# Attention scores in whole float32 products, a third turned buffer, and a new order

## The chip, the cores and the metric

The kernel runs on one core of a Trainium2 chip. The metric is the device time of one execution in microseconds (us). Three runs of the kernel before took 922.01, 923.61 and 915.67 us; the median is 922.01. The engines are TensorE (PE, with its weight loads as PEld), VectorE (DVE), ScalarE (ACT), GpSimd (POOL) and SyncE (SP), which issues the DMAs. Each works through its own queue in order.

## The reference

The inputs are q, k and v of 8 batches, 8 heads, 576 positions and 64 dimensions, and the weights of a gated MLP. All is float32.

```
scores = (q @ k^T) / sqrt(64)
thresh = max(scores, axis=-1) - tau
scores = where(scores >= thresh, scores, -1e9)
attn   = exp(scores - max(scores));  attn = attn / (sum(attn) + 1e-9)
x      = attn @ v                      # heads side by side: (8, 576, 512)

h = gelu_tanh(x @ w_in);  u, v = halves of h
v = layer_norm(v) * g_ln
g = u * (w_sg @ v + b_sg)              # w_sg mixes the 576 positions
out = x + g @ w_out
```

The threshold makes the scores delicate: a score close to the threshold is kept or dropped whole, so the products of q and k are made to float32 precision.

## The kernel before

The work is 32 pairs of heads (`attention(n)`, a pair n is two heads of a batch) and 8 batches of the MLP (`moe(b)`, after each four pairs). Every operation is recorded as a step in a plan, and a list of numbers, `ORDER`, says in which order the steps are issued; `PLACES` says which of the 8 banks of PSUM a step takes. The order of issue is the order in each engine's queue. Attention of later pairs is woven into the MLP of earlier batches.

In a pair, the queries are cut into four blocks of 128 for each head (i = 0 to 3) and a tail of 64 for both heads together (i = 4). A step of scores (`scores`, L583 to L594) writes two heads at once: head 0 from partitions 0 to 63 of q and k, head 1 from 64 to 127, in two halves of 288 keys each. It takes four banks. The tail step (`tail_scores`, L596) uses a copy of q's tail with zeros, so that 128 rows hold both heads, and takes two banks.

For 31 of the pairs q and k are split: q is loaded and scaled (L553, POOL), its rounded part qh is cast by ACT (`hi_part`, L543), the remainder ql is taken by POOL (`lo_part`, L549), the same for k, and POOL copies the tails of qh and ql (L558). The scores are the sum of three products in the type fp32r: qh kh, qh kl and ql kh. Pair 0 alone (`WHOLE_SCORES = 1`) multiplies q and k whole, in float32.

Behind a step of scores follows a chain. DVE takes the row maxima, negated, from the banks (L610). POOL subtracts the threshold offset (L614) and makes the difference for the exponential (L618). ACT selects from the banks into a tile p (L628), which empties the banks for the next step, and takes the exponential (L634). DVE turns blocks of 32 by 32 into a tile pt (L685). Half of pt travels to DRAM and back to other partitions (L695, L702), in two parts: u = 0 holds query blocks 0 and 1, u = 1 the rest. There is one buffer for each part, pt0 and pt1, so the transposes of pair n+1 wait until PE has multiplied part u of pair n. PE multiplies pt with v (`values`, L715), and DVE scales the sums (L723, L725). ACT and POOL then make the two parts of x for the MLP (L730, L733, L736).

The MLP's products are fp32r, with the operands split in the same way, and recorded in pieces of four matmuls (L809). Between early steps stand 16 steps with products of a constant tile (L1044), which keep PE at work.

Of the kernel before, what the change touches and what calls it, by code (L numbers as in the profile page):

```python
# [30 lines left out]
WHOLE_SCORES = 1  # L31

ORDER = [int(i) for i in """
    160 16 162 17 18 161 41 163 19 165 166 167 176 42 178 177 168 43 44 170 179 173 169 184 246 61 215 193 181 45 216
    217 0 244 46 62 174 245 194 195 140 219 10 63 180 251 196 198 47 171 64 175 65 51 81 71 252 247 248 7 13 204 6 205
    206 201 185 207 91 21 208 218 31 197 14 182 66 172 186 209 212 183 4 254 265 72 220 255 256 202 267 221 266 333
    335 249 250 73 187 164 199 213 257 268 214 262 334 210 12 11 270 200 203 189 259 22 1 282 211 23 228 284 67 188
    273 24 223 229 25 82 340 5 3 68 224 83 258 269 32 84 283 26 222 85 341 69 2 120 190 285 304 9 191 230 74 305 27 70
    92 86 287 290 336 75 93 33 286 94 192 48 28 293 76 233 232 49 226 225 95 34 306 338 337 29 231 87 227 274 260 308
    307 88 238 424 288 263 52 271 422 294 96 295 97 77 309 89 30 239 296 275 297 35 264 301 298 36 291 272 310 130 236  # L40
    237 235 234 37 98 90 343 99 302 50 78 253 261 104 299 344 345 53 423 38 425 100 339 346 276 79 101 240 292 39 429
    8 351 241 278 277 40 300 303 354 80 348 426 347 243 289 371 107 355 356 372 352 317 357 242 105 54 312 373 102 362
    359 311 374 318 313 375 55 379 108 430 376 319 358 56 103 57 280 281 279 58 15 382 321 320 59 315 314 383 384 322
    316 380 60 385 106 393 387 390 766 110 113 363 386 109 432 394 434 433 360 349 324 326 768 327 361 377 328 435 395
    116 323 325 364 437 397 396 350 353 398 391 365 111 428 767 436 399 381 392 388 389 378 112 427 406 440 366 367
    438 769 342 400 329 401 441 330 770 460 332 331 462 461 407 402 114 117 443 463 445 408 444 118 369 368 773 446
    370 468 465 448 482 447 449 410 409 411 471 483 774 464 115 141 451 473 472 404 772 474 403 405 475 484 416 450
    476 479 452 776 442 439 855 142 856 857 477 466 131 486 480 778 415 414 777 413 412 453 417 481 469 119 454 485
    478 779 771 418 781 487 470 784 419 862 456 455 780 420 421 495 132 488 467 787 431 788 496 789 489 121 826 782
    511 785 490 491 497 143 133 790 458 792 459 457 144 122 498 500 499 512 804 795 493 858 827 806 828 805 123 863  # L50
    807 124 125 791 126 134 561 528 492 812 809 830 796 494 808 529 815 505 145 146 817 135 946 503 504 816 502 127
    859 786 136 783 813 793 810 818 501 506 20 128 823 545 507 508 820 819 147 797 794 150 944 824 951 865 562 866 509
    513 825 129 510 514 530 531 829 945 563 546 148 515 516 532 517 533 518 519 520 547 831 534 151 821 521 800 594
    535 522 523 536 152 595 524 602 564 537 153 814 947 548 799 798 775 549 839 525 526 603 538 539 550 540 867 565
    527 868 551 541 552 840 542 869 610 577 553 870 873 554 822 841 555 556 543 578 876 801 803 596 557 566 611 877
    832 878 544 567 597 558 612 802 879 871 559 811 568 154 833 884 880 860 560 569 604 598 843 579 605 842 834 844
    580 885 581 613 599 626 618 881 835 570 640 627 849 582 600 583 601 137 584 585 586 149 861 845 846 847 837 571
    619 572 952 614 615 633 620 587 573 606 588 872 607 155 886 621 882 874 616 634 589 574 590 608 575 591 576 609
    622 138 592 617 623 1035 836 848 838 641 593 628 156 624 642 635 643 625 636 629 139 948 875 644 637 893 883 894
    895 850 896 630 897 851 638 887 898 904 157 901 902 905 906 647 915 631 903 916 648 632 907 661 639 649 852 650  # L60
    899 1033 888 662 917 908 909 912 645 954 651 900 918 1034 913 919 663 914 910 920 654 854 675 664 158 956 955 891
    889 864 853 928 668 655 911 957 962 959 929 921 646 656 657 665 658 669 930 965 967 652 1040 159 958 676 677 670
    659 660 666 653 1036 667 966 671 678 689 890 892 968 949 950 682 683 969 1037 1041 690 922 923 973 970 672 679 673
    680 960 691 932 924 931 681 674 982 983 692 933 684 984 1004 1005 985 685 938 971 926 927 987 990 1038 1006 986
    963 1008 961 993 925 693 686 988 974 972 991 694 1007 995 1373 937 936 934 939 994 1009 731 935 687 996 710 975
    1371 997 940 998 1043 964 992 1044 1001 711 703 941 1045 999 1002 943 953 712 1046 704 1010 1000 989 1047 942 1017
    717 713 1003 1018 1048 1051 718 1054 976 688 732 1055 1056 1372 1039 1374 733 734 719 977 978 720 1019 695 735
# [1032 lines left out]
```

## Time and profile before

| | |
|---|---|
| median of three runs | 922.01 us |
| profiled execution | 916.05 us, span 914.3 us |
| PE busy | 827.9 us (91%), 9260 matmuls |
| ACT busy | 684.5 us (75%) |
| DVE busy | 644.7 us (71%) |
| POOL busy | 598.2 us (65%) |
| granted TensorE clock, mean | 0.968 |

Busy times are of one profiled execution, and they overlap between engines. The time of a matmul in the profile runs from its start to the end of its pipeline, so neighbours overlap and a group's busy time is less than its count times its mean. The distance from start to start tells how fast the work goes through. Idle time of an engine is put down to what ended it.

### The profile page before, as it was taken

The page shows a single profiled execution, that of the slowest core. Times are in us where ns is not written, and L with a number is a line of the kernel's source. Part 1 is how long each engine was busy: PE and PEld are TensorE (multiplying, and loading weights), DVE is VectorE, ACT ScalarE, POOL GpSimd, SP SyncE. Part 2 cuts the span into 40 slices and gives each one's busy share as a digit, 9 for nine tenths or more (in the row PEclk, how much of TensorE's full clock was granted, in tenths as well). Part 3 has the DMA queues.
Part 4 walks back from the last instruction along what each step waited for, and adds up shares of the span by engine and source line. Part 5 has one row for each costly group of instructions (what it writes and reads, how often), then busy time and mean ns, then how long its engine had stood idle before and what let it go on. Part 6 is the DMA issues. An engine that isn't in the chain of part 4 may idle for free.

```text
span 914.3 us, 24350 instructions
## 1 busy us (share of the span) xinstructions
PE 827.9 (91%) x9260; PEld 717.7 (78%) x9260; DVE 644.7 (71%) x1142; ACT 684.5 (75%) x1425; POOL 598.2 (65%) x1053
## 2 busy tenths in 40 slices
PE   6877888998799989998899998999889999999898
PEld 4546667997699867988699876888679987898788
DVE  6896988763877657874777758776586758777165
ACT  6888787974977769985788757877589768887171
POOL 5586578673866668665676658666596648764373
PEclk9897989999989999999899999999999999999999
DMA  7878735684447854677347854688556773567401
GB/s 284 223 215 222 216 99 144 182 216 133 135 129 196 221 154 114 191 191 215 104 135 174 230 142 113 161 216 233 136 136 158 208 203 92 140 188 204 111 15 59
DMA packets 207288, 151.73 MB, mean 166 GB/s; under 512 B 32833, under 2 KB 188481, under 8 KB 207170
## 3 DMA queue, kind: packets, MB, share of 16 engines
q1 hardware_dynamic: 207170, 150.17, 60.8%
q8 instruction: 73, 1.20, 0.5%
q14 instruction: 45, 0.37, 0.1%
HBM read 97.68 MB, written 52.43 MB: 164 GB/s over the span
## 4 chain that ended last, share of the span: by engine, by line
PE 40%; POOL 16%; DVE 12%; DMA 11%; SPq 9%; ACT 8%; issue 6%; DVEq 0%; POOLq 0%; ACTq 0%
PE all_banks L809 23%; PE all_banks L715 8%; PE all_banks L592 7%; DMA pt<-swb 4%; SPq L702 3%; DVE pt L685 3%; DVE columns L610 3%; POOL vv L917 3%; ACT p L628 2%; DMA ir<-ird 2%; POOL z L930 2%; SPq L656 2%; ACT p L634 2%; DMA ird<-ir 2%; SPq L695 2%
## 5 line engine op out<-in xcount | busy, mean ns | idle before, releaser
L610 DVE TENSOR_REDUCE columns<-all_banks 128x1 f32<-128x576 f32 x288 | 205.8, 744 | 79.4 <-PE all_banks L592 67.1
L628 ACT ACTIVATE p<-all_banks,columns 128x576 f32<-128x576 f32 x288 | 202.6, 736 | 69.0 <-POOL columns L614 68.4
L685 DVE STREAM_TRANSPOSE pt<-p 128x576 f32<-128x576 f32 x288 | 206.0, 752 | 48.5 <-PE all_banks L715 35.5
L634 ACT ACTIVATE p<-p,columns 128x576 f32<-128x576 f32 x288 | 220.8, 770 | 3.1 <-POOL columns L618 1.5
L715 PE MATMUL all_banks<-pt,rv 64*64 64x128 f32 (+1 forms) x4608 | 165.8, 293 | 15.8 <-DMA pt<-swb 10.8
L715 PEld LDWEIGHTS all_banks<-pt,rv 64*64 64x64 f32 x4608 | 148.2, 137 | 30.1 <-issue 14.8
L614 POOL TENSOR_SCALAR columns<-columns 128x2 f32<-128x2 f32 (+1 forms) x160 | 54.4, 340 | 135.8 <-DVE columns L610 132.5
L809 PE MATMUL all_banks<-wsh,z 128*128 128x288 f32 (+2 forms) x512 | 116.6, 307 | 11.6 <-DVE uu L788 5.7
L809 PE MATMUL all_banks<-x,wi 128*128 128x288 f32 (+2 forms) x720 | 114.9, 304 | 4.9 <-DVE vv L788 2.9
L809 PE MATMUL all_banks<-wi,x 128*128 128x512 f32 (+1 forms) x424 | 112.3, 406 | 4.9 <-POOL x L733 2.1
L809 PEld LDWEIGHTS all_banks<-x,wi 128*128 128x128 f32 x720 | 102.8, 193 | 12.3 <-DVE vv L788 3.6
L809 PE MATMUL all_banks<-gh,wo 128*128 128x288 f32 (+1 forms) x480 | 104.3, 299 | 0.1
L592 PE MATMUL all_banks<-kh,qh 64*128 64x288 f32 x496 | 80.2, 355 | 23.8 <-ACT p L628 19.4
L809 PEld LDWEIGHTS all_banks<-wsh,z 128*128 128x128 f32 x512 | 86.0, 192 | 18.8 <-DVE uu L788 6.9
L1017 POOL TENSOR_TENSOR ot<-ot,x 128x288 f32<-128x288 f32 x112 | 90.5, 815 | 10.5 <-ACT ot L1026 8.9
L809 PEld LDWEIGHTS all_banks<-wi,x 128*128 128x128 f32 (+1 forms) x424 | 75.8, 188 | 26.2 <-POOL x L733 4.6
L592 PEld LDWEIGHTS all_banks<-kh,qh 64*128 64x128 f32 x496 | 44.5, 187 | 57.0 <-ACT p L628 33.2
L733 POOL TENSOR_TENSOR x<-ir,x 128x576 fp32r<-128x576 f32 x32 | 45.8, 1430 | 62.1 <-ACT x L730 60.4
L809 PEld LDWEIGHTS all_banks<-gh,wo 128*128 128x128 f32 x480 | 78.7, 188 | 5.2 <-issue 3.0
L809 PE MATMUL all_banks<-wsl,z 128*128 128x288 f32 (+2 forms) x256 | 76.2, 302 | 0.0
L809 PE MATMUL all_banks<-gl,wo 128*128 128x288 f32 (+1 forms) x240 | 69.5, 296 | 0.0
L592 PE MATMUL all_banks<-kh,ql 64*128 64x288 f32 x496 | 58.6, 294 | 0.1
(182 smaller groups left out, 1544.1 us busy)
## 6 DMA issues: line engine op xcount, KB each, us to landing
rv<-in_vP SPq DMA_DIRECT2D x32, 576.0 KB
swb<-pt SPq DMA_DIRECT2D x64, 180.0 KB
swb<-pt SPq DMA_DIRECT2D x32, 360.0 KB
pt<-swb SPq DMA_DIRECT2D x64, 180.0 KB
pt<-swb SPq DMA_DIRECT2D x32, 360.0 KB
rq<-in_qT SPq DMA_DIRECT2D x32, 288.0 KB
rk<-in_kT SPq DMA_DIRECT2D x32, 288.0 KB
swa<-pt SPq DMA_DIRECT2D x32, 288.0 KB
```

The source lines that it names most:

```text
L592: nc.tensor.matmul(st["s", h, i][:, a, 0:HALF], st[q][rows, i * P:(i + 1) * P], st[k][rows, a * HALF:(a + 1) * HALF], start=(j == 0), stop ...
L610: return lambda: nc.vector.tensor_reduce(nm, st["s", h, i][:, :, 0:HALF], AX.XY, ALU.max, negate=True)
L614: return lambda: nc.gpsimd.tensor_scalar(nt, nm, toff, 1.0, ALU.subtract, ALU.mult)
L628: nc.scalar.activation(halves(st["p", h, i]), st["s", h, i][:, :, 0:HALF], AF.Prelu, bias=columns_of(i)[1][:, h:h + 1], alpha=BIG)
L634: return lambda: nc.scalar.activation(st["p", h, i], st["p", h, i], AF.Exp, bias=columns_of(i)[2][:, h:h + 1], accum_out=l_of[part][:, c:c ...
L685: nc.vector.transpose(out, st["p", h, i].rearrange("p (j x) -> p j x", x=BLK))
L702: nc.sync.dma_start(turned(u)[rows, :, e], st["sw", u][src].rearrange("p (c w) -> p c w", c=PAIRS))
L715: nc.tensor.matmul(st["acc"][h * D:(h + 1) * D, r, :, c0:c0 + w], v[rows, c, h], turned(u)[rows, c, :, h * w:(h + 1) * w], start=(c == 0), ...
L733: nc.gpsimd.tensor_tensor(xl_of[b, hp], st["ir"], xh_of[b, hp], ALU.subtract)
L809: nc.tensor.matmul(st["acc"][0:rows[0]] if rows else st["acc"], w, x, start=(j == 0), stop=(j == n - 1))
L917: nc.gpsimd.tensor_tensor(st["v", i], st["v", i], g_bc[0:rows], ALU.mult)
L1017: return lambda: nc.gpsimd.tensor_tensor(o(), o(), x[b, m][:, ts_], ALU.add)
```

## The change

The scores of all pairs are made as pair 0's were: q and k whole in float32, one product, no parts. `hi_part`, `lo_part` and the copies of their tails go; what stays is the scaling of q and two copies of its tail into one of two kept tiles with zeros (`tails`). q and k get two raw buffers each, by the parity of the pair. The turned blocks get three buffers of the larger width, taken in turn by (2n + u) mod 3. The threshold on POOL becomes a difference of two tiles, with the offset held in two columns, where it was a tile minus a scalar. `ORDER` and `PLACES` are new.

```
-WHOLE_SCORES = 1
-
 ORDER = [int(i) for i in """
...
-    kpool = ctx.enter_context(tc.tile_pool(name="kpool", bufs=1))
...
-    columns = cpool.tile([P, 4 + GROUPS * COLS], F32, name="columns")
-    tau_sb, qscale, toff, mhalf = (columns[:, c:c + 1] for c in range(4))
+    columns = cpool.tile([P, 8 + GROUPS * COLS], F32, name="columns")
+    toff = columns[:, 0:2]
+    tau_sb, qscale, mhalf = (columns[:, c:c + 1] for c in range(2, 5))
...
-    qz = [cpool.tile([P, P], F32R, name=f"qz{x}") for x in "hl"]
-    for z in qz:
-        nc.gpsimd.memset(z.bitcast(F32), 0.0)
+    tails = [cpool.tile([P, P], F32, name=f"tails{k}") for k in range(2)]
+    for z in tails:
+        nc.gpsimd.memset(z, 0.0)
...
         def load(name, src):
-            pool, tag = (kpool, f"{name}h0") if whole_s else (raws, f"raw{name}")
-
-            def f():
-                st[name] = pool.tile([P, S], F32, tag=tag, name=f"r{name}{n}")
+            def f():
+                st[name] = raws.tile([P, S], F32, tag=f"raw{name}{part}", name=f"r{name}{n}")
                 nc.sync.dma_start(st[name], src)
             return f
...
-        def hi_part(name):
-            def f():
-                st[name + "h"] = kpool.tile([P, S], F32R, tag=f"{name}h{part}", name=f"{name}h{n}")
-                nc.scalar.activation(st[name + "h"], st[name], AF.Copy)
-            return f
-
-        def lo_part(name):
-            def f():
-                st[name + "l"] = kpool.tile([P, S], F32R, tag=f"{name}l{part}", name=f"{name}l{n}")
-                nc.gpsimd.tensor_tensor(st[name + "l"], st[name], st[name + "h"], ALU.subtract)
-            return f
...
+        def q_tails(h):
+            def f():
                 rows = slice(h * D, (h + 1) * D)
...
+                nc.gpsimd.tensor_scalar(tails[part][rows].rearrange("p (g h r) -> p h g r", g=RG, h=2)[:, h],
+                                        st["q"][rows, MAIN:S].rearrange("p (g r) -> p g r", g=RG), 1.0, 0.0, ALU.mult, ALU.add)
+            return f
...
         def scores(i):
             def f():
                 for h in range(2):
                     st["s", h, i] = banks(2)
-                terms = [("q", "k")] if whole_s else [("qh", "kh"), ("qh", "kl"), ("ql", "kh")]
-                for j, (q, k) in enumerate(terms):
-                    for a in range(2):
-                        for h in range(2):
-                            rows = slice(h * D, (h + 1) * D)
-                            nc.tensor.matmul(st["s", h, i][:, a, 0:HALF], st[q][rows, i * P:(i + 1) * P],
-                                             st[k][rows, a * HALF:(a + 1) * HALF], start=(j == 0), stop=(j == len(terms) - 1))
+                for a in range(2):
+                    for h in range(2):
+                        rows = slice(h * D, (h + 1) * D)
+                        nc.tensor.matmul(st["s", h, i][:, a, 0:HALF], st["q"][rows, i * P:(i + 1) * P],
+                                         st["k"][rows, a * HALF:(a + 1) * HALF], start=True, stop=True)
             return f
...
-            terms = [(st["qt"], st["k"])] if whole_s else [(qz[0], st["kh"]), (qz[0], st["kl"]), (qz[1], st["kh"])]
             for a in range(2):
-                for j, (q, k) in enumerate(terms):
-                    nc.tensor.matmul(sc[:, a, 0:HALF], q, k[:, a * HALF:(a + 1) * HALF], start=(j == 0), stop=(j == len(terms) - 1))
+                nc.tensor.matmul(sc[:, a, 0:HALF], tails[part], st["k"][:, a * HALF:(a + 1) * HALF], start=True, stop=True)
...
         def threshold(i):
             nm, nt, _ = columns_of(i)
-            return lambda: nc.gpsimd.tensor_scalar(nt, nm, toff, 1.0, ALU.subtract, ALU.mult)
+            return lambda: nc.gpsimd.tensor_tensor(nt, nm, toff[:, 0:1] if i == NM else toff, ALU.subtract)
...
         def turned(u):
             if ("pt", u) not in st:
-                st["pt", u] = ptp.tile([P, CHUNKS * WIDTHS[u]], F32, tag=f"pt{u}", name=f"pt{u}_{n}")
+                st["pt", u] = ptp.tile([P, CHUNKS * WIDTHS[1]], F32, tag=f"pt{(2 * n + u) % 3}", name=f"pt{u}_{n}")[
+                    :, 0:CHUNKS * WIDTHS[u]]
...
```

The order of the instructions on the engines follows from `ORDER`. Three places show it. In the rows, a number behind a name is a buffer's number, "x4" counts equal matmuls in a row, and lines are those of the kernel in question. A float32 matmul is one row here and two instructions in the profile.

PE in the middle of the run, in the kernel before: a tail step of scores (L601), then part of a gate unit (L809), then one main step (L592).

```order
L601 MATMUL all_banks<-kh_4704,qzh 128x288
L601 MATMUL all_banks<-kl_4796,qzh 128x288
L601 MATMUL all_banks<-kh_4704,qzl 128x288
L601 MATMUL all_banks<-kh_4704,qzh 128x288
L601 MATMUL all_banks<-kl_4796,qzh 128x288
L601 MATMUL all_banks<-kh_4704,qzl 128x288
L809 MATMUL all_banks<-wsl_108,z_1_4480 128x288
L809 MATMUL all_banks<-wsh_104,z_1_4480 128x288
L809 MATMUL all_banks<-wsh_105,z_2_4552 128x288
L809 MATMUL all_banks<-wsl_109,z_2_4552 128x288
L592 MATMUL all_banks<-kh_5044,qh_5040 128x288 x4
L592 MATMUL all_banks<-kl_5108,qh_5040 128x288 x4
L592 MATMUL all_banks<-kh_5044,ql_5063 128x288 x4
```

The same kind of place now: a main step (L554), a tail step (L561), MLP products between (L770), and a main step of the next pair.

```order
L554 MATMUL all_banks<-rk_4651,rq_4611 128x288 x4
L770 MATMUL all_banks<-wi_742,x_4325 128x512 x3
L770 MATMUL all_banks<-wi_564,x_4637 128x512
L561 MATMUL all_banks<-rk_4651,tails_110 128x288 x2
L770 MATMUL all_banks<-wi_564,x_4637 128x512 x2
L770 MATMUL all_banks<-wi_612,x_4915 128x512 x3
L770 MATMUL all_banks<-wi_810,x_5101 128x512 x3
L770 MATMUL all_banks<-x_4325,wi_355 128x288 x3
L770 MATMUL all_banks<-x_4637,wi_440 128x288
L770 MATMUL all_banks<-x_4325,wi_355 128x288 x3
L770 MATMUL all_banks<-x_4637,wi_440 128x288
L554 MATMUL all_banks<-rk_4871,rq_4912 128x288 x4
```

Three rows of a main step became one, six of a tail step became one, and steps of scores stay spread between pieces of the MLP.

POOL in the kernel before, around the subtractions of one pair (L549) with thresholds (L614) and differences (L618) behind them.

```order
L618 TENSOR_TENSOR columns<-columns 128x2
L549 TENSOR_TENSOR ql_5397<-rq_5191,qh_5328 128x576
L1017 TENSOR_TENSOR ot_0_2_5372<-ot_0_2_5372,x_4123 128x288
L614 TENSOR_SCALAR columns<-columns 128x1
L614 TENSOR_SCALAR columns<-columns 128x2
L992 TENSOR_TENSOR gl_1_0_5478<-uu_1_1_5001,gh_1_0_5374 128x288
L1017 TENSOR_TENSOR ot_0_3_5362<-ot_0_3_5362,x_4343 128x288
L558 TENSOR_SCALAR qzh<-qh_5328 64x4x16 x2
```

POOL now, around the scaling of one pair's q (L531) and the copies of its tail (L536); the threshold is L574, the difference L578.

```order
L574 TENSOR_TENSOR columns<-columns 128x2
L531 TENSOR_SCALAR rq_4611<-rq_4611,columns 128x576
L978 TENSOR_TENSOR ot_0_3_4720<-ot_0_3_4720,x_3772 128x288
L536 TENSOR_SCALAR tails_110<-rq_4611 64x4x16
L578 TENSOR_TENSOR columns<-columns 128x2
L978 TENSOR_TENSOR ot_0_3_4720<-ot_0_3_4720,x_3772 128x288
L574 TENSOR_TENSOR columns<-columns 128x2
L578 TENSOR_TENSOR columns<-columns 128x2
L536 TENSOR_SCALAR tails_110<-rq_4611 64x4x16
```

The subtractions are gone from the queue in which the thresholds stand, and a pair has two copies of tails in place of four.

DVE in the kernel before, where the turned blocks of pair 14 begin (L685) and the sums of pair 13 are scaled (L723).

```order
L685 STREAM_TRANSPOSE pt_14_5187<-p_1_0_4992 128x18x32
L610 TENSOR_REDUCE columns<-all_banks 128x1 x2
L685 STREAM_TRANSPOSE pt_14_5187<-p_0_0_4990 128x18x32
L685 STREAM_TRANSPOSE pt_14_5187<-p_0_1_5075 128x18x32
L685 STREAM_TRANSPOSE pt_14_5187<-p_1_1_5077 128x18x32
L723 TENSOR_TENSOR ir_5017<-all_banks,ir_5017 128x4x4x32
```

DVE now, at the same pairs (transposes L646, scaling L684).

```order
L646 STREAM_TRANSPOSE pt_14_4412<-p_1_1_4417 128x18x32
L646 STREAM_TRANSPOSE pt_14_4600<-p_0_4_4500 128x36x16
L749 SCALAR_TENSOR_TENSOR uu_1_2_4602<-gtu_1_2_4498,all_banks 128x288
L646 STREAM_TRANSPOSE pt_14_4600<-p_1_2_4483 128x18x32
L646 STREAM_TRANSPOSE pt_14_4600<-p_1_3_4593 128x18x32
L684 TENSOR_TENSOR ir_4415<-all_banks,ir_4415 128x4x4x32
```

Transposes of the second part of pair 14 (pt_14_4600) now stand ahead of the scaling of pair 13; before, only those of the first part did here.

## Rows read from the trace of the kernel before

**Rows 1.** The page's busy us, share of the span and instructions of each engine.

```profile
PE 827.9 (91%) x9260; PEld 717.7 (78%) x9260; DVE 644.7 (71%) x1142; ACT 684.5 (75%) x1425; POOL 598.2 (65%) x1053
```

**Rows 2.** By stretch: us; busy us of PE, PEld, DVE, ACT, POOL; granted clock; DMA.

```profile
100.00:350.00 250.00, 227.50 (x2542) 197.43 (x2542) 181.44 (x317) 189.84 (x395) 170.96 (x294) 0.95 0.61 163
350.00:850.00 500.00, 471.26 (x5496) 416.19 (x5496) 352.79 (x630) 389.52 (x823) 331.66 (x602) 0.98 0.63 169
...
0.00:100.00 100.00, 72.34 (x732) 51.55 (x732) 81.25 (x134) 80.89 (x160) 64.48 (x117) 0.91 0.81 233
```

**Rows 3.** Waits of PE: us in total, times, longest us.

```profile
PE all_banks L592 <- ACT p L628: 19.4, 28, 2.8
PE all_banks L715 <- DMA pt<-swb: 10.8, 12, 2.1
...
PE all_banks L601 <- ACT p L628: 4.7, 4, 2.6
PE all_banks L1044 <- ACT p L628: 4.6, 2, 3.2
...
PE all_banks L715 <- DMA pt<-swa: 3.5, 4, 1.2
```

**Rows 4.** Timeline of PE, split scores: start us, us, line, operands, count.

```profile
401.19 0.29 PE L601 MATMUL all_banks<-kh,qzh 128*128 128x288 f32 x1
...
401.85 0.29 PE L601 MATMUL all_banks<-kh,qzl 128*128 128x288 f32 x1
401.99 0.43 PE L809 MATMUL all_banks<-wsh,z 128*128 128x288 f32 x2
...
403.94 0.53 PE L592 MATMUL all_banks<-kh,qh 64*128 64x288 f32 x4
...
404.56 0.43 PE L592 MATMUL all_banks<-kh,ql 64*128 64x288 f32 x4
404.93 0.40 PE L809 MATMUL all_banks<-wsh,z 128*128 128x288 f32 x1
```

**Rows 5.** Timeline of PE, pair 0, whole scores.

```profile
10.73 1.24 PE L601 MATMUL all_banks<-rk,qt 128*128 128x288 f32 x4 [1.12 <-ACT p L628]
11.89 1.73 PE L592 MATMUL all_banks<-rk,rq 64*128 64x288 f32 x8
...
15.48 1.24 PE L592 MATMUL all_banks<-rk,rq 64*128 64x288 f32 x8
16.79 1.56 PE L1044 MATMUL all_banks<-warm 128*128 128x256 f32 x6
```

**Rows 6.** Instructions of line L592: duration ns min/median/max, first and last start.

```profile
L592 PE MATMUL all_banks<-kl,qh x496: 288/291/438, 19.0 to 834.0; 64*128 64x288 f32 x166
...
L592 PE MATMUL all_banks<-rk,rq x32: 402/507/846, 5.7 to 16.3; 64*128 64x288 f32 x32
```

**Rows 7.** Groups of ACT: count, busy us, mean ns, idle before, releaser.

```profile
L543 ACT ACTIVATE qh<-rq 128x576 fp32r<-128x576 f32 x31 | 21.0, 677 | 5.0 <-POOL rq L553 5.0
```

**Rows 8.** Groups of POOL, same columns.

```profile
L549 POOL TENSOR_TENSOR ql<-rq,qh 128x576 fp32r<-128x576 f32 x31 | 45.5, 1468 | 5.5 <-ACT qh L543 5.3
...
L549 POOL TENSOR_TENSOR kl<-rk,kh 128x576 fp32r<-128x576 f32 x31 | 44.2, 1426 | 0.7 <-ACT kh L543 0.4
L614 POOL TENSOR_SCALAR columns<-columns 128x2 f32<-128x2 f32 x128 | 43.5, 340 | 115.8 <-DVE columns L610 113.0 <-DVE ir L647 1.7
...
L618 POOL TENSOR_TENSOR columns<-columns 128x2 f32<-128x2 f32 x128 | 27.2, 214 | 4.8
...
L558 POOL TENSOR_SCALAR qzl<-ql 64x64 fp32r<-64x64 f32 x62 | 15.8, 256 | 2.8
```

**Rows 9.** Waits of all engines: us in total, times, longest us.

```profile
DVE pt L685 <- PE all_banks L715: 35.5, 15, 5.3
```

**Rows 10.** Groups of the chain behind the scores, on DVE and ACT, from the page.

```profile
L610 DVE TENSOR_REDUCE columns<-all_banks 128x1 f32<-128x576 f32 x288 | 205.8, 744 | 79.4 <-PE all_banks L592 67.1
L628 ACT ACTIVATE p<-all_banks,columns 128x576 f32<-128x576 f32 x288 | 202.6, 736 | 69.0 <-POOL columns L614 68.4
```

More of the change, by code (lines that the diff above doesn't have):

```diff
@@ L377, in threshold_offset @@
         at("tau", 1, lambda: nc.vector.tensor_scalar(qscale, tau_sb, 0.0, SCALE, ALU.is_ge, ALU.mult))
-        at("tau", 2, lambda: nc.vector.tensor_scalar(toff, tau_sb, 0.0, -BIG, ALU.is_lt, ALU.mult))
-        at("tau", 3, lambda: nc.vector.tensor_tensor(toff, toff, tau_sb, ALU.subtract))
+        both = tau_sb.broadcast_to([P, 2])
+        at("tau", 2, lambda: nc.vector.tensor_scalar(toff, both, 0.0, -BIG, ALU.is_lt, ALU.mult))
+        at("tau", 3, lambda: nc.vector.tensor_tensor(toff, toff, both, ALU.subtract))
     used = [0]
@@ L538, in v_load @@
             nc.sync.dma_start(st["v"], vP[n])
-        def hi_part(name):
-            def f():
-                st[name + "h"] = kpool.tile([P, S], F32R, tag=f"{name}h{part}", name=f"{name}h{n}")
-                nc.scalar.activation(st[name + "h"], st[name], AF.Copy)
-            return f
-        def lo_part(name):
-            def f():
-                st[name + "l"] = kpool.tile([P, S], F32R, tag=f"{name}l{part}", name=f"{name}l{n}")
-                nc.gpsimd.tensor_tensor(st[name + "l"], st[name], st[name + "h"], ALU.subtract)
-            return f
         def q_scale():
             nc.gpsimd.tensor_scalar(st["q"], st["q"], qscale, 1.0, ALU.mult, ALU.mult)
-        def both_tails(dst, src):
-            for h in range(2):
+        def q_tails(h):
+            def f():
                 rows = slice(h * D, (h + 1) * D)
-                nc.gpsimd.tensor_scalar(dst[rows].rearrange("p (g h r) -> p h g r", g=RG, h=2)[:, h],
-                                        src[rows, MAIN:S].rearrange("p (g r) -> p g r", g=RG), 1.0, 0.0, ALU.mult, ALU.add)
-        def q_zeros(k):
-            return lambda: both_tails(qz[k], st["q" + "hl"[k]].bitcast(F32))
-        def q_tails():
-            qt = st["qt"] = m2.tile([P, HALF], F32, tag="u0", name=f"qt{n}")[:, 0:P]
-            nc.gpsimd.memset(qt, 0.0)
-            both_tails(qt, st["q"])
+                nc.gpsimd.tensor_scalar(tails[part][rows].rearrange("p (g h r) -> p h g r", g=RG, h=2)[:, h],
+                                        st["q"][rows, MAIN:S].rearrange("p (g r) -> p g r", g=RG), 1.0, 0.0, ALU.mult, ALU.add)
+            return f
         at("q_load", load("q", qT[b, 2 * hp:2 * hp + 2].rearrange("h d s -> (h d) s")))
@@ L586, in f @@
                     st["s", h, i] = banks(2)
-                terms = [("q", "k")] if whole_s else [("qh", "kh"), ("qh", "kl"), ("ql", "kh")]
-                for j, (q, k) in enumerate(terms):
-                    for a in range(2):
-                        for h in range(2):
-                            rows = slice(h * D, (h + 1) * D)
-                            nc.tensor.matmul(st["s", h, i][:, a, 0:HALF], st[q][rows, i * P:(i + 1) * P],
-                                             st[k][rows, a * HALF:(a + 1) * HALF], start=(j == 0), stop=(j == len(terms) - 1))
+                for a in range(2):
+                    for h in range(2):
+                        rows = slice(h * D, (h + 1) * D)
+                        nc.tensor.matmul(st["s", h, i][:, a, 0:HALF], st["q"][rows, i * P:(i + 1) * P],
+                                         st["k"][rows, a * HALF:(a + 1) * HALF], start=True, stop=True)
             return f
@@ L884, in new @@
                 if last:
-                    pool, w, tag = (ppool, S, f"p{k}") if i % 2 else (raws, S, f"raw{'qk'[k]}")
+                    pool, w, tag = (ppool, S, f"p{k}") if i % 2 else (raws, S, f"raw{'qk'[k]}0")
                 else:
```

25 lines of the change are left out of this document (8 added, 17 removed), and 412 rows, old and new, of the table ORDER.

## The prediction

> **What bounds the kernel now.** I read the page's busy shares first, then the table by stretch of time, then what TensorE (PE) waited for, and last the timeline of single steps. The shares name PE: 827.9 us busy of a span of 914.3, the next engine (ACT) 684.5 [rows 1]. A busy PE is not yet a bound, so I look at where it is busy. From 350 to 850 us it is busy 471.26 of 500 us, 94%; from 100 to 350 us 227.50 of 250, 91%; only in the first 100 us, where PE is busy 72.34, do DVE (81.25) and ACT (80.89) stand above it [rows 2]. Inside the busy stretches the matmuls stand close: six start between 401.19 and 401.99, one every 0.13 us [rows 4]. So after the first 100 us the kernel is nearly a queue on PE, and what PE still loses are waits of which the largest by far is for ACT's select, the step that empties the score banks: 19.4 us ahead of the main score products, 4.7 ahead of the tail ones, 4.6 ahead of warm-up products, 28.7 together; then 14.3 for turned blocks to come back from DRAM (10.8 + 3.5) [rows 3]. The profiled execution took 916.05 us, 1.78 more than its span; the median of the runs shown is 922.01. The sum below is made against 916.05, and I add the 5.96 us to the median at its end.
>
> **The score products (the main term).** For 31 of the 32 pairs, four main steps and one tail step change. A main step before is 12 fp32r instructions: two heads side by side, three terms, two halves. The timeline shows one from 403.94 to the start of the next work at 404.93; its last row ends at 404.56 + 0.43 = 404.99, so it is busy for 1.05 us [rows 4]. The whole product exists in this trace too, because pair 0 is already done so: one whole float32 matmul is two instructions, a main step is eight, and its row takes 1.24 us (from 15.48) [rows 5]. The reason is in the durations: a whole instruction takes 402 ns at least, an fp32r one of the same 288 columns 288 ns [rows 6], so each of the fewer instructions streams longer. Difference: 0.19 us a step, 124 steps: **+23.6 us**. The tail step before is six instructions from 401.19 to 401.85 + 0.29, 0.95 us [rows 4]; whole it is four, 1.24 us [rows 5]: 0.29 us, 31 times: **+9.0 us**. Sum +32.6 us of PE.
>
> Bounds: if the longer last instruction of each step (402 less 291 = 0.11 us) is covered by the next step's start, it is 0.08 x 124 + 0.18 x 31 = 15 us. If start to start is the right reading (15.48 to 16.79 is 1.31 against 0.99; 10.73 to 11.89 is 1.16 against 0.80), it is 0.32 x 124 + 0.36 x 31 = 51 us. I take 32.6, since the start of the warm-up at 16.79 may hold a wait of its own.
>
> Here a rule speaks against the change. The Trainium skill, "FP8 and Floating Point Precision", section TensorE Precision Notes, says that a true FP32 product takes four passes through the array (all four combinations of high and low parts). By that rule four passes stand where three were: an estimate from it is a third on top of 1.05 and 0.95 us, 0.35 x 124 + 0.32 x 31 = 53 us, the upper end of what the rows give. The rows of pair 0 decide for less, and the sum goes by them.
>
> **What is removed.** ACT loses two casts a pair, of q and of k, at 21.0 us for each, 42 us of its 684.5 [rows 1, 7]. POOL loses two subtractions (45.5 + 44.2 us) and two of the four tail copies (15.8), about 105 us of 598.2 [rows 1, 8]. The threshold becomes a tile difference; the nearest row of that form and width is L618, 214 ns against 340 now [rows 8]: 0.126 us, 160 times, 20 us of POOL. None of this is PE time. Its worth is only through waits: a threshold of 0.3 us that stands in POOL's queue behind a subtraction of 1.4 us, or a select behind a cast of 0.68 us on ACT, holds the banks and so PE. Neither the casts nor the subtractions stand among what PE waited for [rows 3], so the longer preparation that falls away is worth nothing by itself.
>
> **What is added.** q and k get two raw buffers; the load of pair n+2 now has to wait for the scores of pair n. A pair lasts some 914/32 = 28.6 us, and what lies between load and use is one DMA, one scaling and two copies of 0.26 us [rows 8]; I cost it at nothing, covered by the pair between. If the cover goes, each late pair costs PE those few us.
>
> **Third buffer for turned blocks.** DVE waits 35.5 us in 15 places for PE to release such a buffer [rows 9]. In the changed order transposes do stand ahead of the previous pair's scaling where they could not before. DVE is busy 644.7 of 914.3 [rows 1], so this is no gain of DVE; it can only bring maxima and transposes earlier, and so shorten PE's waits for selects and for blocks.
>
> **What returns.** The waits that the relief can reach are the 28.7 and the 14.3 us above, 43 us. Bounds: nothing (the chain of one step, two maxima of 0.744, threshold, two selects of 0.736 [rows 10], gets 0.13 shorter and its product 0.19 longer, so unqueued it does not shrink), or all 43. The chain's own steps (3.3 us) remain, only queueing in front of them falls, on engines that lose 6% (ACT) and about 21% (POOL, with the threshold) of their work: I take half, 22 us. Forecast: 916.05 + 32.6 - 22 = 927 us, against the median 922 + 11 = 933; between the two I put **928 us**.
>
> The clock: the granted share was 0.91, 0.95 and 0.98 in the three stretches [rows 2], 12.5 us at the one and 10 us at the other of the long ones if PE had never fallen to 1.2 GHz; that loss stands beside the waits, and what returns of it is in the half.
>
> **The rivals.**
>
> 1. **The relief wins (faster).** Place: PE's waits on select and on blocks. If all 43 us go and the first 100 us, where DVE and ACT carry the load, lose the four pairs' casts (4 x 1.36 = 5 us), it is 922 + 32.6 - 48 = 907, and with the low price of the products (15 us) 889. It decides once more than 33 us come back. For it: the start is not bound by PE, POOL loses a fifth, the third buffer is used. Against it: 33 us have to be earned from a PE that is at 94% in the largest stretch. Time 905, chance 0.25.
> 2. **Nothing returns (clearly slower).** The waits are latencies of a chain that does not shrink, and PE is simply longer: 922 + 33 = 955 (937 to 973 by the bounds). For it: DVE, the first link (67.1 us waited for score products; POOL then 113.0 us for the maxima [rows 8, 10]), loses no work. Chance 0.22.
> 3. **The change does not do what it says:** whole products of the two heads no longer run side by side between other work, so a step's eight instructions cost twice: 124 x 1 us more, about 1050. Against it: pair 0's eight take 1.24 us in a stretch between warm-up products [rows 5]. Chance 0.03.
>
> **How the numbers follow.** The forecast (half returns) has 0.47 and its own range is 916 to 942; the remaining 0.03 lies outside all of these. One per cent, 9 us, is about what a measurement here can tell from no change. Faster by over 1% (below 913): nearly all of rival 1, 0.24. Within 1% (913 to 931): half of the forecast and the edges of the rivals, 0.35. Slower: the other half, rival 2 and rival 3, 0.41. The range that leaves out no more than a fifth runs from 902, inside rival 1, to 952, inside rival 2.
>
> **What would show it.** In the changed profile the score lines on PE should hold about 33 us more busy time in fewer instructions (32 main and tail instructions a pair, plus four), with 402 ns as the shortest; ACT about 42 and POOL about 120 us less busy; PE's idle time should fall from 86 us (914.3 - 827.9) to about 65; the waits on select should about halve. If PE is as idle as before, rival 2 holds; if its idle time is under 45 us, rival 1. A main step much under 1.2 us, or the start losing 20 us or more, would make the prediction wrong in its terms.

## The result, and the profile after

The changed kernel takes **889.51 us**, the median of four runs (886.58 to 890.17); the kernel before takes 918.84 beside it, the median of the three runs above and a fourth (914.81 to 923.61). The ratio is 0.967, with a 95% interval of 0.961 to 0.973. The prediction said 928 us and a range of 902 to 952: the change is faster, and by more than the range allowed.

The profiled execution has a span of 887.7 us, where before it had 914.3. First the busy line of the page, to be set beside [rows 1].

```profile
PE 837.5 (94%) x8702; PEld 687.6 (77%) x8702; DVE 641.8 (72%) x1142; ACT 646.1 (73%) x1363; POOL 473.9 (53%) x928
```

PE works 9.6 us more than before, and the span is 26.6 us shorter: its idle time fell from 86.4 to 50.2 us. ACT lost 38 us of work and POOL 124, much as worked out ahead (42 and 125).

Then the stretches, to be set beside [rows 2]. The columns are the stretch, its length, the busy us of PE, PEld, DVE, ACT and POOL, the granted clock of TensorE, and DMA.

```profile
0.00:100.00 100.00, 85.30 (x684) 55.22 (x684) 79.46 (x137) 78.11 (x156) 45.86 (x102) 0.88 0.84 235
100.00:350.00 250.00, 236.51 (x2542) 196.75 (x2540) 191.39 (x337) 191.31 (x402) 146.59 (x276) 0.99 0.62 169
350.00:850.00 500.00, 482.88 (x5241) 403.25 (x5238) 351.51 (x627) 363.25 (x779) 259.70 (x524) 1.00 0.63 169
```

PE is busier in each stretch, and from 100 us on the clock hardly falls (0.95 and 0.98 before, 0.99 and 1.00 now); in the first 100 us it is a little lower than before, 0.88 against 0.91. The clock has two levels, 1.2 and 2.4 GHz, so a mean granted clock of 0.968 over 914.3 us, as before, is 58 us at the lower one (twice 0.032 of the span), and the mean after, 0.985 over 887.7 us, is 27 us. A second profiled execution of the changed kernel (experiment 8) has 0.990 over nearly the same span, 887.9 us, so 18 us: the time at the lower level varies by some 9 us between executions that take equally long.

Now the score products. The first two rows are the busy time of L592 and of L601 alone over the whole span before, each with its count; the next two are those of L554 and L561 after. (The second figure is that of the weight loads.)

```profile
0.00:915.00 915.00, 153.60 (x1520) 115.47 (x1520) 0.97 0.61 166
0.00:915.00 915.00, 33.87 (x190) 28.55 (x190) 0.97 0.61 166
```

```profile
0.00:888.00 888.00, 175.19 (x1024) 99.74 (x1024) 0.98 0.63 171
0.00:888.00 888.00, 39.20 (x128) 23.71 (x128) 0.98 0.63 171
```

187.5 us became 214.4: the products cost **26.9 us** more, in fewer instructions. A main step by itself is seen in the timeline of PE after (start us, us, line, operands, count):

```profile
371.83 1.24 PE L554 MATMUL all_banks<-rk,rq 64*128 64x288 f32 x8
373.00 4.64 PE L676 MATMUL all_banks<-pt,rv 64*64 64x128 f32 x144
377.57 1.24 PE L554 MATMUL all_banks<-rk,rq 64*128 64x288 f32 x8
378.74 0.53 PE L770 MATMUL all_banks<-wsh,z 128*128 128x288 f32 x2
```

From its start to that of the next work it takes 1.17 us, against 0.99 before [rows 4]. Nothing stands between these four visits of PE.

Last, what PE waited for after (us in total, times, longest us), to be set beside [rows 3].

```profile
PE all_banks L676 <- DMA pt<-swb: 7.8, 8, 1.5
PE all_banks L554 <- ACT p L588: 5.3, 7, 1.6
PE all_banks L561 <- ACT p L588: 3.0, 2, 2.7
...
PE all_banks L786 <- ACT p L588: 1.8, 1, 1.8
...
PE all_banks L676 <- ACT p L588: 1.4, 2, 0.9
...
PE all_banks L770 <- DVE uu L749: 1.0, 1, 1.0
...
PE all_banks L770 <- DVE vv L749: 0.6, 2, 0.4
```

The last two are waits of the MLP's products for DVE. Their lines before, which no row ahead of the prediction showed, were these:

```profile
PE all_banks L809 <- DVE uu L788: 5.7, 4, 1.9
...
PE all_banks L809 <- DVE vv L788: 4.0, 5, 1.3
```

The waits for a select, 28.7 us before, come to 11.5 in these rows, and those for blocks, 14.3 before, to 7.8. The wait of DVE for a turned buffer [rows 9], 35.5 us before, is down to one of 1.3 us:

```profile
DVE pt L646 <- PE all_banks L676: 1.3, 1, 1.3
```

So the span can be added up: scores +26.9, the rest of PE's busy time -17.3 (9.6 less 26.9), idle time -36.2, together -26.6. What has to be explained is why so much came back.

### The profile page after: what moved, and what is told of

Read it like the earlier page. It is cut to its first block, busy times and chain, and to the rows that moved or that the text cites. A ratio compares the mean times of both kernels' runs of the same rounds, so it can differ in the third digit from the quotient of the medians.

```text
span 887.7 us, 23063 instructions
## 1 busy us (share of the span) xinstructions
PE 837.5 (94%) x8702; PEld 687.6 (77%) x8702; DVE 641.8 (72%) x1142; ACT 646.1 (73%) x1363; POOL 473.9 (53%) x928
## 4 chain that ended last, share of the span: by engine, by line
PE 28%; DMA 5%; SPq 4%; DVE 4%; POOL 3%; ACT 3%; issue 3%; DVEq 0%; POOLq 0%; ACTq 0%
PE all_banks L770 17%; PE all_banks L554 5%; PE all_banks L676 5%; DMA pt<-swb 3%; SPq L663 2%; PE all_banks L561 1%; SPq L656 1%; ACT p L594 1%; POOL ot L978 1%; DMA swa<-pt 1%; SPq L616 1%; DVE columns L570 1%; ACT p L588 1%; DVE vv L749 1%; DVE pt L646 1%
## 5 line engine op out<-in xcount | busy, mean ns | idle before, releaser
L570 DVE TENSOR_REDUCE columns<-all_banks 128x1 f32<-128x576 f32 x288 | 206.5, 747 | 88.2 <-PE all_banks L554 66.1
L646 DVE STREAM_TRANSPOSE pt<-p 128x576 f32<-128x576 f32 x288 | 209.1, 755 | 16.9 <-ACT p L594 10.9
L554 PE MATMUL all_banks<-rk,rq 64*128 64x288 f32 x1024 | 175.2, 436 | 10.9 <-ACT p L588 5.3
L676 PE MATMUL all_banks<-pt,rv 64*64 64x128 f32 (+1 forms) x4608 | 156.4, 285 | 15.9 <-DMA pt<-swb 7.8
L676 PEld LDWEIGHTS all_banks<-pt,rv 64*64 64x64 f32 x4608 | 141.2, 133 | 34.6 <-issue 16.2
L574 POOL TENSOR_TENSOR columns<-columns 128x2 f32<-128x2 f32 (+1 forms) x160 | 34.6, 216 | 206.8 <-DVE columns L570 200.7
L554 PEld LDWEIGHTS all_banks<-rk,rq 64*128 64x128 f32 x1024 | 99.7, 188 | 58.3 <-ACT p L588 17.6
L770 PE MATMUL all_banks<-wsh,z 128*128 128x288 f32 (+2 forms) x512 | 114.8, 305 | 2.6 <-ACT z L884 1.1
L770 PE MATMUL all_banks<-x,wi 128*128 128x288 f32 (+2 forms) x720 | 114.1, 300 | 1.8 <-DVE uu L749 1.0
L770 PE MATMUL all_banks<-wi,x 128*128 128x512 f32 x424 | 112.4, 402 | 2.6 <-DVE ir L686 1.5
L770 PEld LDWEIGHTS all_banks<-x,wi 128*128 128x128 f32 x720 | 100.8, 188 | 14.5 <-issue 5.4
L770 PE MATMUL all_banks<-gh,wo 128*128 128x288 f32 (+1 forms) x480 | 103.6, 297 | 1.6 <-DVE ir L686 1.5
L770 PEld LDWEIGHTS all_banks<-wsh,z 128*128 128x128 f32 x512 | 85.0, 190 | 12.5 <-issue 5.4
L770 PEld LDWEIGHTS all_banks<-wi,x 128*128 128x128 f32 x424 | 74.0, 184 | 26.5 <-issue 4.7
L770 PEld LDWEIGHTS all_banks<-gh,wo 128*128 128x128 f32 x480 | 78.7, 188 | 7.6 <-issue 2.7
L770 PE MATMUL all_banks<-wsl,z 128*128 128x288 f32 (+2 forms) x256 | 76.3, 303 | 0.0
L770 PE MATMUL all_banks<-gl,wo 128*128 128x288 f32 (+1 forms) x240 | 70.6, 300 | 0.8 <-POOL gl L953 0.8
L684 DVE TENSOR_TENSOR ir<-all_banks,ir 128x512 f32<-128x512 f32 x32 | 21.9, 685 | 62.9 <-PE all_banks L676 28.7
```

The source lines that it names most:

```text
L554: nc.tensor.matmul(st["s", h, i][:, a, 0:HALF], st["q"][rows, i * P:(i + 1) * P], st["k"][rows, a * HALF:(a + 1) * HALF], start=True, stop ...
L570: return lambda: nc.vector.tensor_reduce(nm, st["s", h, i][:, :, 0:HALF], AX.XY, ALU.max, negate=True)
L574: return lambda: nc.gpsimd.tensor_tensor(nt, nm, toff[:, 0:1] if i == NM else toff, ALU.subtract)
L646: nc.vector.transpose(out, st["p", h, i].rearrange("p (j x) -> p j x", x=BLK))
L676: nc.tensor.matmul(st["acc"][h * D:(h + 1) * D, r, :, c0:c0 + w], v[rows, c, h], turned(u)[rows, c, :, h * w:(h + 1) * w], start=(c == 0), ...
L684: nc.vector.tensor_tensor(main, acc[:, :, 0:MAINQ].rearrange("p g (i x) -> p g i x", x=BLK), main, ALU.mult)
```

## The experiments

The change has four parts: the products (and with them what ACT and POOL lose), the third buffer, the threshold, and the order. The theories were these. **Theory R**, relief: ACT and POOL are freer, so the banks come free sooner. **Theory O**, order: the instructions stand in better places, and relief alone is worth little. **Theory B**, the third buffer lets transposes run ahead and that is the gain, came up on the way. (In the expectations quoted below, "relief" or "room" is theory R and "order" is theory O; theories with a number belong to that run alone.) Beside the experiments the kernel before stood at 914.4 to 915.3 us.

**1. The new products in the old order.** The old list of numbers is laid on the steps that remain. Two turned buffers, the threshold as before. Ten loads and tail steps had to be moved, because of the two raw buffers.

```diff
-ORDER, PLACES = the new lists
+ORDER, PLACES = the old lists, without the casts, subtractions and copies that are gone
-tag=f"pt{(2 * n + u) % 3}"
+tag=f"pt{u}"
-nc.gpsimd.tensor_tensor(nt, nm, toff[:, 0:1] if i == NM else toff, ALU.subtract)
+nc.gpsimd.tensor_scalar(nt, nm, toff[:, 0:1], 1.0, ALU.subtract, ALU.mult)
```

> Whole products for all pairs with two raw buffers of q and k, but two buffers for turned blocks, the threshold as tile minus scalar and the order of the kernel before (casts and subtractions taken out of it, ten loads and tail steps moved behind the last use of their buffer). If the relief of ACT and POOL is what pays (theory relief), most of the gain is here already: 895 to 905 us against about 919 before. If the new order with its third buffer pays (theory order), the old order keeps PE's waits, and the longer products show: 930 to 945 us.

945.76 us (941.82 to 949.65), ratio 1.036 [1.032, 1.040], 31 us slower than before and just above the range for theory O. Its page shows PE at 859.6 us of 940.0, so 80.4 us idle, where it was 86.4 before the change. The products cost what they cost on PE, and the room on ACT and POOL gives only these 6 us back: theory R falls for this order.

**2. With the third buffer and the tile difference as well**, still in the old order. Only `ORDER` and `PLACES` now differ from the changed kernel.

```diff
-ORDER, PLACES = the new lists
+ORDER, PLACES = the lists of experiment 1
```

> The changed kernel with the old order alone: whole products, third buffer, threshold as a tile difference, but the instructions in the order of the kernel before. Theory relief: within 5 us of the changed kernel's 889.5. Theory order: 920 us or more, since a buffer that the order does not use early is worth little. A result between, near 905, would share the gain out in halves.

940.84 us (936.75 to 945.13), ratio 1.029 [1.025, 1.034]. From here to the changed kernel the same instructions in the same buffers get about 51 us faster by their order (the old order was made for other steps; no third order was tried). The busy line of its page, and then three waits of PE:

```profile
PE 858.9 (91%) x8702; PEld 697.8 (74%) x8702; DVE 641.6 (68%) x1142; ACT 649.5 (69%) x1363; POOL 474.6 (51%) x928
```

```profile
PE all_banks L554 <- ACT p L588: 15.4, 18, 2.3
PE all_banks L676 <- DMA pt<-swb: 8.5, 12, 2.2
...
PE all_banks L1005 <- ACT p L588: 4.3, 2, 3.0
```

ACT and POOL are as free as in the changed kernel (646.1 and 473.9 there), and yet the select is waited for 15.4 us ahead of the main products, where the changed kernel has 5.3. Its mean clock is 0.969, as before the change: 58 us of 938.9 at the lower level. The buffer itself did its work here: with two buffers (experiment 1) DVE waited 22.9 us in 11 places for one, with three it does not wait for one at all, and yet no more than 5 us were won.

The 51 us can be divided. PE's idle time falls from 80.0 us (938.9 less 858.9) to 50.2, which is 30 us. Its busy time, for the same instructions, falls from 858.9 to 837.5, which is 21 us. Of the 58 us at the lower level PE is at work in 51.4, and in the changed kernel in 26.4 of 27.3 (16.1 of 18.5 in its second profiled execution). Half of the difference, 12 to 18 us, is an estimate of what the clock has in those 21.

**3. The new order with two turned buffers.** In the new order 86 of the 288 transposes stand ahead of the products with v that release such a buffer. They, and 13 steps that hang on them, are moved to right behind those products; nothing else is moved.

```diff
-tag=f"pt{(2 * n + u) % 3}"
+tag=f"pt{u}"
-ORDER = the new list
+ORDER = the new list, 99 steps of it later
```

> The changed kernel with two turned buffers (one for each part) in place of three. 86 of the 288 transposes stand in the new order ahead of the products with v that release such a buffer; they, and the 13 steps that hang on them, are moved to right behind those products, and nothing else is moved. Theory 1 (the order gives the gain, and needs the third buffer for it): the 86 transposes come late, blocks come back late, PE waits for them, and 15 to 35 us of the gain go: 905 to 925 us. Rival (the order gives it by where products and selects stand, the buffer adds little, as in the old order, where the third buffer and the tile difference together gave 5): 889 to 898 us.

962.07 us (959.84 to 966.46), ratio 1.051 [1.048, 1.055]: 73 us over the changed kernel, twice the largest price expected, and 16 us over the old order with two buffers. How a missing buffer gets to PE is seen around the end of pair 13. DVE, first in the changed kernel (L570 takes the maxima of the main step just made, L646 transposes for pair 14, L684 scales pair 13):

```profile
373.10 1.42 DVE L570 TENSOR_REDUCE columns<-all_banks 128x1 f32<-128x576 f32 x2 [0.81 <-PE all_banks L554]
374.44 1.66 DVE L646 STREAM_TRANSPOSE pt<-p 128x576 f32<-128x576 f32 x2
376.03 0.42 DVE L749 SCALAR_TENSOR_TENSOR uu<-gtu,all_banks 128x288 f32<-128x288 f32 x1
376.37 1.60 DVE L646 STREAM_TRANSPOSE pt<-p 128x576 f32<-128x576 f32 x2
378.07 0.69 DVE L684 TENSOR_TENSOR ir<-all_banks,ir 128x512 f32<-128x512 f32 x1
```

and with two buffers (L645, L683), with the idle time and what ended it in brackets:

```profile
400.33 0.45 DVE L754 SCALAR_TENSOR_TENSOR gtu<-gtu,all_banks 128x288 f32<-128x288 f32 x1 [1.12 <-ACT gtu L741]
403.87 2.10 DVE L645 STREAM_TRANSPOSE pt<-p 128x576 f32<-128x576 f32 x3 [3.09 <-PE all_banks L675]
405.89 1.39 DVE L570 TENSOR_REDUCE columns<-all_banks 128x1 f32<-128x576 f32 x2
...
410.44 0.65 DVE L683 TENSOR_TENSOR ir<-all_banks,ir 128x512 f32<-128x512 f32 x1
```

PE with two buffers, over the same time:

```profile
400.44 1.24 PE L554 MATMUL all_banks<-rk,rq 64*128 64x288 f32 x8
401.61 4.79 PE L675 MATMUL all_banks<-pt,rv 64*64 64x128 f32 x144
408.38 2.92 PE L554 MATMUL all_banks<-rk,rq 64*128 64x288 f32 x8 [1.98 <-ACT p L588]
411.22 0.85 PE L769 MATMUL all_banks<-wsh,z 128*128 128x288 f32 x2
```

It is the very sequence of four visits shown above for the changed kernel, and it comes apart in three steps. DVE stands 3.09 us at a transpose until PE has multiplied the old blocks. The maxima (L570) queue behind that transpose: they start 4.2 us after their main step has ended (405.89 after 401.68), where in the changed kernel they follow it at once (373.10 after 373.07). So threshold and select are late, and PE waits 1.98 us for banks. And then the main step takes 2.92 us instead of 1.24, mostly because the granted clock falls 0.5 us into it, as the stretches of this kernel show:

```profile
401.00:408.00 7.00, 5.39 (x150) 4.56 (x146) 4.13 (x7) 3.13 (x8) 0.97 (x4) 1.00 0.64 154
408.00:415.00 7.00, 6.62 (x24) 5.24 (x25) 5.88 (x11) 5.09 (x10) 2.42 (x7) 0.56 0.81 223
```

24 matmuls in the second stretch, at 0.56. The clock is not all of it: at half the clock a step of 1.17 us would take 2.34 us to the start of the next work, and this one takes 2.84; its weight loads wait once more, 0.3 us, for the second select. Over the whole run the mean clock is 0.956, 85 us of 960.9 at the lower level. In this trace each of the 13 falls of the clock between 100 us and the last product comes during or shortly after a wait of PE of 1.2 us or more; yet of its 15 waits of over 1.5 us in that time, 4 are followed by no fall. The sum of waits is no longer led by the select alone:

```profile
PE all_banks L554 <- ACT p L588: 28.1, 18, 3.6
PE all_banks L554 <- DVE ir L685: 14.7, 6, 4.4
PE all_banks L769 <- DVE ir L685: 14.5, 6, 5.1
```

The scaling of the sums (L685) stands behind the late transposes too, and holds the banks of the sums. So buffer and order are each worth little or less than nothing alone, and together (with the tile difference) 56 us: old order with two buffers 945.8, with three (and the tile difference) 940.8; new order with two 962.1, with three 889.3. That holds for these places of the 86 transposes; others, later ones or ones that a planner would choose for two buffers, were not tried.

**4. Relief without anything else.** Two kernels have the order of before. In the first POOL's subtractions and its copies of the low tails are gone, and each product uses the high parts three times, so PE has the same work; the low parts of the scores are left out. The second has only the threshold as a tile difference.

```diff
-terms = [("q", "k")] if whole_s else [("qh", "kh"), ("qh", "kl"), ("ql", "kh")]
+terms = [("q", "k")] if whole_s else [("qh", "kh")] * 3
```

> The kernel before without the remainders: POOL's two subtractions and two tail copies a pair are left out (about 105 us of POOL), and the three fp32r products of a step all read the rounded parts of q and k, so PE's work stays as it was. It leaves out the low parts of the scores. If relief of POOL pays in the old order, 900 to 908 us; if it needs an order made for it (theory order, as the 945.8 us of the whole products in the old order suggest), 911 to 919 us.

```diff
-nc.gpsimd.tensor_scalar(nt, nm, toff, 1.0, ALU.subtract, ALU.mult)
+nc.gpsimd.tensor_tensor(nt, nm, toff[:, 0:1] if i == NM else toff, ALU.subtract)
```

> The kernel before with only its threshold changed, from tile minus scalar to tile difference. Theory 1 (in the old order, relief of POOL comes back only in small part): 20 us less of POOL are worth 0 to 5 us: 909 to 915. Rival (the threshold stands in the chain of each step of scores, and 0.126 us a step are won in 160 steps): 20 us, 895 us.

909.46 us, ratio 0.993 [0.990, 0.995], and 913.25 us, ratio 0.997 [0.994, 1.000]. The relief of POOL was worth 5 us in the old order, the cheaper threshold about 2, at the edge of what these runs can tell.

**5. The threshold taken back** in the changed kernel.

```diff
-nc.gpsimd.tensor_tensor(nt, nm, toff[:, 0:1] if i == NM else toff, ALU.subtract)
+nc.gpsimd.tensor_scalar(nt, nm, toff[:, 0:1], 1.0, ALU.subtract, ALU.mult)
```

> The changed kernel with the threshold as tile minus scalar again: 160 instructions of POOL 0.126 us longer each, on the chain from maxima to select. Theory relief: chains hold PE, so 5 to 10 us slower than 889.5. Theory order: the order has room for it, under 3 us.

893.54 us, ratio 0.978 [0.974, 0.982]. The changed kernel itself was run again in another study (below) at 0.971 [0.968, 0.974], and the intervals just touch: a loss of 4 to 6 us, not settled.

**6. The room given back.** If the new order lives on the freed room of ACT and POOL, then work of the same length, put back without any use, must cost time there. In the first kernel it stood between the load and the first use of q and k, in place on them.

```diff
+        def dead_cast(name):
+            return lambda: nc.scalar.activation(st[name], st[name], AF.Copy)
+        def dead_sub(name):
+            return lambda: nc.gpsimd.tensor_tensor(st[name], st[name], zero.broadcast_to([P, S]), ALU.subtract)
```

> The changed kernel with dead work in its place: for pairs 1 to 31 a copy of q and of k in place on ACT (0.68 us each, 42 us in all) and a subtraction of zero in place on POOL (1.4 us each, 90 us in all), between load and first use, so ACT and POOL are as busy as before; products, order and buffers stay. Theory relief: most of the gain goes, 910 to 920 us. Theory order: the gain stays, 890 to 897 us.

930.81 us, ratio 1.017 [1.012, 1.022]. This one tells little, for PE waited directly for the dead work, 15.5 us for that on q and 6.8 for that on k:

```profile
PE all_banks L572 <- POOL rq L542: 15.5, 8, 3.7
...
PE all_banks L572 <- POOL rk L542: 6.8, 6, 2.0
```

So in three further kernels the dead work stands behind the last use of q and k, where no product needs it (pairs 0 to 29): the copies alone (41 us of ACT), the subtractions alone (71 us of POOL, less than the 124 that went), and both.

> The changed kernel with dead work on ACT alone: for pairs 0 to 29 a copy of q and of k in place (0.68 us each, 41 us in all), issued behind the last product that reads them and ahead of the load that overwrites them, so that no product waits for it. If the new order lives on the room that ACT gained (theory room), 5 to 15 us slower than 889.5. If the order itself is the gain and the room is not needed (theory order), 0 to 3 us.

> The same on POOL alone: a subtraction of zero in place from q and from k (1.1 to 1.4 us each, 66 to 84 us in all) behind their last product. Theory room: POOL's queue holds the thresholds, so 10 to 25 us slower than 889.5. Theory order: 0 to 4 us, and then the 41 us of the dead work ahead of the products came from products that waited for late operands.

> The changed kernel with both kinds of removed work put back as dead work behind the last use of q and k: two copies a pair on ACT (41 us in all, alone +11.5) and two subtractions a pair on POOL (alone +21). Theory 1 (the order lives on the room of both engines, and each gives its own share): the sum, 889.5 + 32.5 = 922 us, or more where the two add up in one chain. Rival (both fill one and the same slack, which is gone once): no more than the larger, 905 to 912 us.

901.01 us (0.985 [0.982, 0.989]), 910.55 us (0.993 [0.989, 0.996]) and 922.02 us (1.007 [1.004, 1.009]). Over 889.3 that is 12, 21 and 33 us: the two add up. With both, PE's waits show the select back ahead of the main products (L571 here), and the blocks later:

```profile
PE all_banks L693 <- DMA pt<-swb: 13.1, 14, 2.3
PE all_banks L571 <- ACT p L605: 12.2, 18, 2.1
PE all_banks L578 <- ACT p L605: 4.7, 3, 4.0
```

So work of this size on ACT and POOL costs 33 us in the new order, where in the old one 103 us less of POOL gave some 5. Theory R was not wrong about the place, the select and the blocks, but the room has to be used by an order. That all of the 33 us are the worth of the room is not shown: the dead work also holds the loads that reuse q and k, and with them SyncE's queue. Its longest waits at these loads, in the changed kernel (L523) and with both kinds of dead work (L530):

```profile
SPq L523 <- PE all_banks L554: 18.0, 7, 5.9
SPq L523 <- PE all_banks L561: 17.1, 3, 15.4
```

```profile
SPq L530 <- POOL rk L541: 28.6, 8, 19.6
...
SPq L530 <- POOL columns L591: 24.9, 7, 10.6
SPq L530 <- POOL rq L541: 19.4, 4, 7.7
```

How much of the 33 us comes from there was not taken apart. The subtractions alone show one thing more. PE's idle time rises by 12.4 us and its busy time by 10.6 (848.1 of 910.6), but the mean clock stays at 0.983, 31 us at the lower level against 27. So here waits came back, and busy time grew, with hardly any of it from the clock.

**7. What a microsecond of PE costs now.** Each tail product is made twice: 31 us more of PE, nothing else.

```diff
+                for again in range(2):
+                    nc.tensor.matmul(sc[:, a, 0:HALF], tails[part], st["k"][:, a * HALF:(a + 1) * HALF], start=True, stop=True)
-                nc.tensor.matmul(sc[:, a, 0:HALF], tails[part], st["k"][:, a * HALF:(a + 1) * HALF], start=True, stop=True)
```

> The changed kernel with each tail product of scores made twice: 128 more instructions on PE, 0.24 us each, 31 us in all; nothing else changes. If PE's time is the price in the new order as in the old one (theory PE), 915 to 922 us. If the new order left PE room that the profile does not show as idle (rival), under 905 us.

909.64 us, ratio 0.995 [0.993, 0.998], between the two expectations: 20 us for 31, some 0.65 us for each us. The tail products (L562 here, 39.20 us in the changed kernel) hold 31.3 us more:

```profile
0.00:907.00 907.00, 70.51 (x256) 48.22 (x256) 0.98 0.62 167
```

PE's idle time falls from 50.2 to 40.3 us. PE sets the end in the changed kernel too, but a third of an added product still falls into its gaps.

**8. The changed kernel again**, on the chip of experiments 3, 4 (second) and 6 (both).

> The changed kernel itself once more, so that the next three runs have it on their own chip. On record it took 889.51 us where the kernel before took 918.84; where the kernel before takes 914 to 915, as in the other studies, 884 to 893 is expected, a ratio of 0.967 to 0.977.

889.26 us (887.40 to 889.79), ratio 0.971 [0.968, 0.974] to 915.32 us of 23 runs of the kernel before. None of the variants beats it.

## Why the prediction was wrong

- **The score products: right in kind, a little dear.** 32.6 us were forecast, 26.9 are in the records. The main step was put at 0.19 us more and is 0.18; the tail step was put at 0.29, and L561 rose by 5.3 us in all, 0.17 a pair. The weighing of the rule came out for the row: the Trainium skill, "FP8 and Floating Point Precision", section TensorE Precision Notes, has four passes for a true FP32 product; by it, as an estimate, the main step would be a third dearer, and the trace shows 18% (0.99 to 1.17 us). The four passes themselves are not refuted: the 64 float32 products added in experiment 7 cost 31.3 us, 0.49 us each, and an fp32r product of the same shape starts every 0.13 us [rows 4], so one is 3.7 times the other. What did not hold is the step from there to a third on top of a whole main step.
- **What is removed: right.** 42 us of ACT and 125 of POOL were forecast, 38 and 124 went. That this is worth nothing by itself was nearly right in the old order (experiments 1 and 4) and wrong in the new one (up to 33 us, experiment 6).
- **The raw buffers: right.** No load of q or k stands among the larger waits of PE after.
- **"What returns": the step that failed.** It allowed half of 43 us, and no more than all of them, and took the relief for the cause. In the listed rows 24 us of those 43 did return, close to the half; but that is luck, for with the relief alone, in the old order, PE's idle time fell by 6 us in all. And 53 us came back in all (26.9 + 26.6). The other 29 or so were in no term of the sum. 12 us are further idle time of PE (36.2 less 24): the waits of the MLP for uu and vv fell from 9.7 to 1.6 us, and some 6 us are warm-up products that now fill the first wait for k, and win nothing; other rows grew. 17 us are PE's own busy time outside the scores. For the last, the clock is the nearest reading: PE was at work in 50.2 of the 58 us at the lower level before, and in 26.4 of the 27 after, so half of 24, 12 us (17 by the second profiled execution). That is an estimate; no run holds the clock up by itself, and the rest has no reading. The text saw the clock, as 12.5 and 10 us of loss, and then let it pass as part of "the half". The two-buffer kernel shows why it cannot pass so: one wait of 1.98 us, and then a stretch at 0.56 that lasts longer than the wait.
- **The third buffer: seen, and priced wrongly.** It was said that transposes now stand ahead of the scaling of the pair before, and that this can only shorten PE's waits. The 35.5 us of DVE [rows 9] were set aside because DVE is not the bound. Yet the maxima queue behind the waiting transpose, and behind the maxima stand threshold, select and PE. With the new order the third buffer is worth 73 us (experiment 3, where 99 steps stand later for want of it); in the old one 5 at most, though DVE's waits for a buffer went there too.
- **The order was taken as neutral.** The rows of the order were shown ahead of the prediction, but no term of it carried a price for them. It is the largest single step of all: 51 us at equal instructions and buffers.
- **The rivals.** "The relief wins" had the right side and, at 905 or, with the low price of the products, 889 us, nearly the right time, but by luck: the old order shows that relief alone does not give it. "Nothing returns", 955 us, is what the change would have been without order and buffer: 941 to 946. The text's own mark, idle time of PE under 45 us for relief and 86 for nothing, gave 50.2 us, near to the first.

Open is which places of the new order carry the gain. Of its 51 us, 30 are idle time of PE and 12 to 18, by the estimate in experiment 2, the clock; whether the clock stayed up because the waits went was not tried by itself, and in experiment 6 waits came back without it.

## What to carry to other kernels

An engine that is 91% busy can still hide tens of microseconds in short waits, and its clock can fall after one, so count the time at the lower clock as a term of its own. When a change comes with a new order, price the order as a part: ask which instruction at the head of a queue can no longer block those behind it, and follow the queue, not only the instruction, to the bound. A buffer, freed room and an order may be worth little one by one and much together, so undo them in pairs before calling one of them the cause.

## What was not expected of the hardware

- The float32 products of a main step cost 1.17 us from start to start, three times as many fp32r products of the same operands 0.99 us: 18% dearer, in eight instructions instead of twelve.
- After PE had been idle for 1.98 us behind products with v of 64 by 64, the granted clock of the 7 us from 408 was 0.56, and a main step took 2.92 us instead of 1.24. Not every wait was followed by a fall: of 15 of over 1.5 us in that trace, 4 were not.
